# Moving z's parts, batch 1's bounds, a product with u and one half step's preparation in the opening of a squared-ReLU attention with a soft mixture of experts

## The chip, the cores and the metric

One core of one Trainium2 chip runs the whole program. The metric is the device time of one execution in microseconds (us); lower is better. TensorE is called PE, ScalarE ACT, VectorE DVE, GpSimd POOL, and SyncE's queue of transfers SP, as the profile does.

## The reference

Eight batches of 2496 tokens. `u` and `v` have 256 columns, `z` has 64. Attention uses `z` for both queries and keys; its result, times `u`, goes into a soft mixture of experts.

```python
scores = scale * np.matmul(z, z.transpose(0, 2, 1))      # scale = 1/2496
attn = np.maximum(scores, 0.0) ** 2
x = (u * np.matmul(attn, v)).reshape(B * S, D)
logits = x @ phi                                         # 32 slots: 8 experts of 4
# softmax over tokens gives slot inputs, two layers per expert, softmax over slots mixes them back
```

## The kernel before, in words

Attention is cut, batch by batch, into chunks of 512 queries. A chunk is walked in ten **half steps**, each with 256 keys. Half steps are numbered through the run; the loop variable is `h` (line 1094). Half steps 0 to 9 are chunk 0, 10 to 19 chunk 1, 20 to 29 chunk 2. The work of half step k is called sc(k), relu(k) and so on here:

- **sc(k)**: PE multiplies z by z into PSUM. For k below 12 (`RAW_SCORES`) it uses raw z in fp32; from 12 on it uses z's two fp16 parts in three pairs of matmuls, which read high and high, high keys and low queries, low keys and high queries, in this order (lines 407 to 420).
- **relu(k), square(k)** on ACT, out of PSUM into a tile `r`.
- **cast(k)**: the high fp16 part `ph`, on POOL or on ACT; **pl(k)**: the low part, `r - ph`, on DVE. Up to k = 21 both go in two halves.
- **y(k)**: DVE transposes `r` for the mirrored chunk, where scores are needed a second time; those later half steps ("turned") fetch it back from memory and need no sc. Half steps 12, 13, 20, 22 and 23 are turned.
- **sums of k**: PE multiplies `ph` and `pl` by v's two parts into `acc`, as high by high, v's low by high, v's high by low. With a preparation between them the sums of a half step are cut in two phases, p0 and p1 (`sums_halves`); else they are whole (`sums_whole`).

Every engine's instructions stay in the order of the program (`InOrder`, line 72). In half step h (up to 17) the program issues p0 of h, then the preparation of h+2 (scores on PE, then relu, square, cast, pl, y), then whatever lies in the list `behind`, then p1 of h. From 19 on it prepares h+3; 18 prepares both 20 and 21. Between p0 and p1 stands a `nop` on POOL (line 645) that passes PE on.

The names the change touches:

- `z_splits[j]` makes z's parts for block j of batch 0: the high part on ACT, the low part on DVE (lines 161 to 166). `FIRST_Z` (line 49) says at the end of which half step. With `FIRST_MEETS` the half steps of chunk 1 meet the blocks 1, 0, 2, 4, 3, so sc(14) needs blocks 1 and 2, sc(16) block 4, sc(18) block 3.
- `landing[h]` is moved into `behind` in half step h. Batch 1's five bounds (a DVE reduction of z times z into `tops`, line 156) land there, then `add_bounds` (a PE matmul over `tops`) and `factors` (four small DVE instructions on its result).
- `finish_chunk` writes chunk 0's result `xg` from `acc`, then multiplies it by u (line 685).
- `prepare_first` and the lines around 1068 to 1089 order the first preparations by hand; `largest` and `scale_v` make v's factor `v_by`.

Of the kernel before, what the change touches and what calls it, by code (L numbers as in the profile page):

```python
# [8 lines left out]
F32 = mybir.dt.float32  # L9
# [9 lines left out]
P = 128  # L19
# [6 lines left out]
QC = 512  # L26
# [5 lines left out]
NP = KT // 4  # L32
NBLK = 16
NRAW = 12
NW_OWN = 7
# [10 lines left out]
)  # L46
FIRST_MEETS = ((0, 1, 2, 3, 4), (1, 0, 2, 4, 3)) + MEETS[0][2:]

FIRST_Z = {8: 1, 10: 2, 11: 4, 13: 3}

RAW_SCORES = 12

FILL = 6, 3

WHOLE, KEEP = 2, 6

ON_ACT = 3, 5, 7

# [25 lines left out]
def attn_soft_moe_kernel(ctx, tc, uT, v, zz, zh, phi, ww, outT):  # L84
    nc = tc.nc

    pe, act, dve, sp, gp = (InOrder(tc, x) for x in (nc.tensor, nc.scalar, nc.vector, nc.sync, nc.gpsimd))
# [82 lines left out]
    def add_bounds(b, ps, js):  # L170
        ones_k = nc.const_aps.tensor(1.0, [P, P], F32)
        for h, rows in enumerate(HALF if b else [slice(0, P)]):
            pe.matmul(ps[:, h, js], ones_k[rows], tops[b % 2][rows, js], start=True, stop=True)

    def factors(b, ps, js):


        n2, by = (t[b % 2][:, js] for t in (norm2, z_by))
        total = ps[:, 0, js]
        if b:  # L180
            dve.tensor_reduce(n2, ps[:, :, js].rearrange("p h j -> p j h"), axis=AX.X, op=ALU.add)
            total = n2
        dve.tensor_scalar(bits(n2), bits(total), EVEN, None, op0=ALU.bitwise_and)
        dve.tensor_scalar(
            bits(by), bits(n2), EVEN, 1, op0=ALU.bitwise_xor, op1=ALU.logical_shift_right
        )
        dve.tensor_scalar_mul(by, by, 2.0**77)
# [29 lines left out]
    def largest(b):  # L217


        root, w = v_by[b % 2], few[b % 2]  # L220
        n2 = norm2[b % 2].unsqueeze(2).to_broadcast([P, NP, 2])
        dve.tensor_scalar(
            bits(root), bits(energy[b % 2]), 1, ROOT, op0=ALU.logical_shift_right, op1=ALU.bitwise_and
        )
        r2 = root.rearrange("p (j i) -> p j i", i=2)
        dve.tensor_tensor_reduce(
            r2, r2, n2, 1.0, 2.0**-120, op0=ALU.mult, op1=ALU.max, accum_out=w[:, 0:1]
        )
# [78 lines left out]
    ut_ = {}  # L307
# [55 lines left out]
    def run(todo):  # L363
        now, todo[:] = todo[:], []
        for f in now:
            f()
# [99 lines left out]
    def prepare_first(k):  # L466

        r = wa.tile([P, 2, QC], F32, tag="r", name=f"r_{k}", bufs=4)
        pend[k] = hi, lo = high_low(k)
        ps, _ = early.pop(k)  # L470

        def parts(t):
            nc.gpsimd.tensor_copy(hi[:, t], r[:, t])
            return lambda: dve.tensor_sub(lo[:, t], r[:, t], hi[:, t])

        return lambda: relu(k, r, ps), lambda: act.activation(r, r, AF.Square), parts, lambda: stage(k, r)
# [23 lines left out]
    def prepare(k):  # L500

        x = halves[k]
        n = x.ch[2]

        if x.turned:
            whole = arriving.pop(k)
            run(middle)
        else:
            r = wa.tile([P, 2, QC], F32, tag="r", name=f"r_{k}", bufs=4)
            ps, m = early.pop(k) if k in early else scores(k)  # L510
            relu(k, r[:, :, :m], ps[:, :, :m])
            act.activation(r[:, :, :m], r[:, :, :m], AF.Square)
            run(middle)
            whole = r[:, :, :m].rearrange("p h (a r) -> p h a r", r=P // 2 if x.borrows else P)
        run(splitting)
        run(turning)
        cast = gp.tensor_copy
        if x.turned or (k <= CATCH + 3 and x.turns and x.at % 3 and k >= 2 * NP):
            cast = act.copy
        pieces = [(whole, slice(0, P), cast)]  # L520
        if x.borrows:
            lent = arriving.pop(k)
            pieces = [(lent, slice(0, P // 2), act.copy), (whole, slice(P // 2, P), dve.tensor_copy)]

        m = QC if x.padded else n

        def halves_of(t):
            return t[:, :, :m].rearrange("p h (a r) -> p h a r", r=P)

        def high():  # L530
            pend[k] = high_low(k)
            for src, cols, cast in pieces:
                cast(halves_of(pend[k][0])[:, :, :, cols], src)

        def low():
            hc, lc = map(halves_of, pend[k])
            for src, cols, _ in pieces:
                dve.tensor_sub(lc[:, :, :, cols], src, hc[:, :, :, cols])

        if x.borrows:  # L540
            pend[k] = high_low(k)
            hc, lc = map(halves_of, pend[k])
            for src, cols, cast in pieces:
                cast(hc[:, :, :, cols], src)
                dve.tensor_sub(lc[:, :, :, cols], src, hc[:, :, :, cols])
        elif k <= CATCH + 3:
            pend[k] = high_low(k)
            hc, lc = map(halves_of, pend[k])
            for t in range(2):
                cast(hc[:, t], whole[:, t])  # L550
                dve.tensor_sub(lc[:, t], whole[:, t], hc[:, t])
        elif x.turned:
            high()
            low()
        else:
            casting.append(high)
            splitting.append(low)
        if x.turns:
            stage(k, r)
        if x.lends:  # L560
            y = turns_sb.tile([P, 4, 2, 2, NS], F32, tag="yd", name=f"yd_{k}", bufs=1)
            dve.transpose(
                y.rearrange("p a j i q -> p i a j q"),
                r.rearrange("p h (a i q) -> p h a i q", i=4, q=NS)[:, :, :, 2:4],
            )
            stores.append((k - 1, lambda: lend(x, y)))
        run(behind)
# [98 lines left out]
    xg_ = {}  # L666

    def finish_chunk(b, ch, acc):
        j, _, n, t0 = ch
        ut = ut_.pop(t0)  # L670
        s = 0
        while s < n:
            q, o = divmod(t0 + s, 1024)
            w = min(n - s, 1024 - o)
            if q not in xg_:
                xg_[q] = wk.tile([P, 2, 1024], F32, tag="xg", name=f"xg_{q}")
            for c in (slice(0, 1), slice(1, 2)) if t0 + n == N else (slice(0, 2),):
                first = t0 == 0
                dve.scalar_tensor_tensor(
                    xg_[q][:, c, o : o + w], acc[:, c, s : s + w], out_by[b % 2][:, j : j + 1],  # L680
                    kept[0][:, c] if first else ut[:, c, s : s + w],
                    op0=ALU.mult, op1=ALU.add if first else ALU.mult,
                )
                if first:
                    dve.tensor_mul(xg_[q][:, :, 0:w], xg_[q][:, :, 0:w], ut)
            if o + w == 1024:
                work.extend(groups(q))
            s += w
# [258 lines left out]

    def load_u(b, ch):
        _, _, n, t0 = ch
        ut = wa.tile([P, 2, QC], F32, tag="ut", name=f"ut_{t0}", bufs=1)  # L950
        q0 = t0 - b * S
        sp.dma_start(
            ut[:, :, :n], uT[b, :, q0 : q0 + n].rearrange("(c p) q -> p c q", p=P)
        )
        ut_[t0] = ut
# [5 lines left out]
    splits, later = {}, {}  # L961
    for b in range(1, B):
        base, order = (b - 1) * 2 * NP * NQ, BLOCKS[b == B - 1]
        z_at = [28, 29, 30, 31, 39]
        v_from = [6, 7, 8, 9, 24, 25, 26, 31, 32, 33]
        v_sq = [17, 18, 19, 20, 28, 29, 30, 32, 33, 33]
        v_high = [43, 41, 41, 42, 42, 43, 44, 44, 45, 45]
        v_low = [47, 42, 43, 44, 45, 46, 48, 49, 50, 51]
        for i, (j, at) in enumerate(zip(order, z_at)):
            splits.setdefault(base + 9 + 2 * i, []).append((load_z, b, j, [base + 12 + 2 * i, base + at]))  # L970
        for i, (start, *steps) in enumerate(zip(v_from, v_sq, v_high, v_low)):
            splits.setdefault(base + start, []).append((load_v, b, i, [base + at for at in steps]))
        later[base + 23] = lambda b=b: add_bounds(b, next_acc(), slice(0, NP))
        later[base + 24] = lambda b=b: factors(b, accs[-1], slice(0, NP))
        later[base + 36] = lambda b=b: largest(b)
        later[base + 39] = lambda b=b: scale_v(b, ms_ps.tile([P, 2, 512], F32, tag="ms", name=f"mx_{b}"))
    landing, fetched = {}, set()
# [2 lines left out]
    def next_acc():  # L980

        accs.append(acc_ps.tile([P, 2, QC], F32, tag="acc", name=f"acc_{len(accs)}"))
        return accs[-1]
# [87 lines left out]
        first_v[i](act if i in ON_ACT else dve)  # L1071
    square2()
    low2 = [parts2(t) for t in range(2)]
    largest(0)
    sums_raw(1, acc_raw, 0, [1])
    scale_v(0, small)
# [9 lines left out]
    dve.tensor_scalar(  # L1086
        raw_by[:, NP:], z_by[0][:, 1:2], z_by[0][:, 1:2], 2.0**-22, op0=ALU.mult, op1=ALU.mult
    )
    prepare(3)
    kept = [own_w.tile([P, 2, QC], F32, tag="own", name="kept", bufs=NW_OWN)]  # L1090
    landing_kept = lambda: act.activation(kept[0], acc_raw, AF.Identity, scale=2.0**22 / S**2)
    landing[KEEP] = [landing_kept]
# [356 lines left out]
```

## Time and profile before

| | |
|---|---|
| median of 3 runs | 1269.56 us (1269.4 to 1270.18) |
| the profiled execution, its own time | 1269.41 us |
| its span, first to last instruction | 1267.6 us |
| PE busy | 1241.6 us, 98% |
| DVE, ACT, POOL busy | 83%, 66%, 18% |
| granted TensorE clock, mean | 0.987 |

The span leaves 1.8 us of the profiled time outside it. A busy share is an average over stages, and matmul ends in the profile are modelled, so PE's pace is read from the starts of its instructions.

### The profile page before, as it was taken

What the parts mean: (1) busy time and instruction counts of PE and PEld (TensorE: products, weight loads), DVE (VectorE), ACT (ScalarE), POOL (GpSimd) and SP (SyncE); (2) the same over time, 40 slices, a digit from 0 to 9 for tenths busy, and PEclk for the clock granted to TensorE, in tenths of its full rate; (3) what the DMA queues carried; (4) which work ended last, traced back from release to release, by engine and by line L of the source; (5) the groups of instructions that cost most, each with busy time, mean ns of one, the idle gap of its engine ahead of it and who ended that gap; (6) DMA issues with size and microseconds to landing.
All of it is one profiled execution on the core that took longest, in us unless ns stands there. A gap on an engine that the chain in (4) does not pass through costs nothing.

```text
span 1267.6 us, 27769 instructions
## 1 busy us (share of the span) xinstructions
PE 1241.6 (98%) x10936; PEld 604.5 (48%) x10937; DVE 1046.0 (83%) x1468; ACT 841.9 (66%) x1143; POOL 229.3 (18%) x234
## 2 busy tenths in 40 slices
PE   9999999999999999999999999999999999999984
PEld 3444454444544444445544444444444455445752
DVE  7988898779978889788987888788987789776563
ACT  7877765767666766577656776577666777564552
POOL 2211032201311032110311123110321113110100
PEclk9999999999999999999999999999999999999995
DMA  6778469773878748784787758786587848989769
GB/s 197 244 211 277 170 190 303 232 238 119 240 263 270 240 126 274 244 235 163 213 276 218 268 149 244 256 255 210 156 277 230 267 142 239 277 278 328 280 272 376
DMA packets 136690, 299.28 MB, mean 236 GB/s; under 512 B 17904, under 2 KB 38896, under 8 KB 124656
## 3 DMA queue, kind: packets, MB, share of 16 engines
q1 hardware_dynamic: 136560, 297.51, 74.0%
q8 instruction: 86, 1.41, 0.5%
q14 instruction: 44, 0.36, 0.1%
HBM read 162.43 MB, written 113.77 MB: 218 GB/s over the span
## 4 chain that ended last, share of the span: by engine, by line
PE 93%; ACT 2%; DVE 2%; DMA 1%; issue 1%; POOL 0%; ACTq 0%; DVEq 0%; POOLq 0%
PE acc L80 76%; PE sc L80 11%; PE lg L80 3%; DMA outT<-ot 1%; PE pf L80 1%; ACT r L80 1%; ACT ot L80 1%; DVE pl L80 1%; PE h L80 1%; PE po L80 0%; DVE y L80 0%; PE acc_raw L80 0%; DVE v L80 0%; DVE xg L80 0%; PE xt L80 0%
## 5 line engine op out<-in xcount | busy, mean ns | idle before, releaser
L80 PE MATMUL acc<-ph,v 64*128 64x512 f16 (+4 forms) x5004 | 923.7, 368 | 0.4 <-POOLq L80 0.3
L80 PEld LDWEIGHTS <-v 64*128 64x128 f16 (+1 forms) x7506 | 467.7, 95 | 521.3 <-issue 38.6
L80 PE MATMUL acc<-pl,v 64*128 64x512 f16 (+5 forms) x2502 | 597.9, 368 | 2.3 <-DVE pl L80 2.3
L80 DVE TENSOR_TENSOR pl<-r,ph 128x1024 f16<-128x1024 f32 (+1 forms) x428 | 475.7, 1123 | 35.0 <-ACT ph L80 25.6
L80 POOL CAST ph<-r 128x1024 f16<-128x1024 f32 (+1 forms) x210 | 224.4, 1072 | 942.7 <-ACT r L80 693.8
L80 ACT ACTIVATE r<-sc 128x1024 f32<-128x1024 f32 (+1 forms) x233 | 220.3, 946 | 234.5 <-PE sc L80 231.9
L80 DVE STREAM_TRANSPOSE y<-r 128x1024 f32<-128x1024 f32 x160 | 198.3, 1239 | 68.9 <-ACT r L80 65.0
L80 ACT ACTIVATE r<-r 128x1024 f32<-128x1024 f32 (+1 forms) x243 | 239.0, 983 | 7.7
L80 ACT CAST ph<-r 128x1024 f16<-128x1024 f32 (+1 forms) x180 | 172.0, 963 | 98.3 <-PE acc L80 60.0
L80 PE MATMUL sc<-z,z 64*128 64x512 f16 x912 | 123.9, 376 | 0.0
L80 PEld LDWEIGHTS <-z 64*128 64x128 f16 x1380 | 69.7, 94 | 72.1 <-DVE z L80 0.3
L80 DVE SCALAR_TENSOR_TENSOR xg<-acc,out_by,ut 128x1024 f32<-128x1024 f32 (+7 forms) x56 | 50.6, 926 | 17.7 <-PE acc L80 17.4
L80 DVE SCALAR_TENSOR_TENSOR v<-vr,v_by,v 128x512 f16<-128x512 f32 (+1 forms) x81 | 60.6, 750 | 0.0
L80 ACT ACTIVATE v<-vr,v_by 128x512 f16<-128x512 f32 (+1 forms) x81 | 53.8, 707 | 7.6 <-DVE v_by L80 7.6
L80 DVE STREAM_TRANSPOSE yd<-r 128x512 f32<-128x512 f32 x36 | 25.5, 709 | 31.2 <-ACT r L80 29.8
L80 PE MATMUL sc<-z 64*128 64x512 f16 (+1 forms) x468 | 50.6, 321 | 0.0
L80 DVE STREAM_TRANSPOSE y<-xg 128x512 f32<-128x512 f32 x72 | 49.4, 686 | 0.0
L80 ACT ACTIVATE vq<-vr 128x512 bf16<-128x512 f32 x73 | 45.5, 623 | 3.6 <-DMA vr<-in_v 3.3
L80 DVE COPY ot<-pf 128x1024 f32<-128x1024 f32 (+2 forms) x21 | 24.1, 1147 | 18.1 <-PE pf L80 14.6
L80 DVE TENSOR_TENSOR pl<-rd,ph 128x512 f16<-128x512 f32 x36 | 24.7, 686 | 14.9 <-ACT ph L80 14.9
L80 ACT COPY ot<-pf 128x1024 f32<-128x1024 f32 (+2 forms) x21 | 20.0, 951 | 22.8 <-PE pf L80 16.4
L80 DVE SCALAR_TENSOR_TENSOR z<-zr,z_by,z 128x512 f16<-128x512 f32 x35 | 25.8, 737 | 0.0
(193 smaller groups left out, 555.9 us busy)
## 6 DMA issues: line engine op xcount, KB each, us to landing
turned<-y SPq DMA_DIRECT2D x320, 256.0 KB, 5.5
r<-turned SPq DMA_DIRECT2D x76, 1024.0 KB, 7.3
xt<-y SPq DMA_DIRECT2D x288, 72.0 KB, 3.9
vr<-in_v SPq DMA_DIRECT2D x80, 256.0 KB, 4.9
outT<-ot SPq DMA_DIRECT2D x17, 1024.0 KB, 7.0
ut<-in_uT SPq DMA_DIRECT2D x31, 512.0 KB, 6.2
lent<-yd SPq DMA_DIRECT2D x144, 64.0 KB, 3.3
rd<-lent SPq DMA_DIRECT2D x36, 256.0 KB, 4.0
```

The source lines that it names most:

```text
L80: return lambda *a, **k: self.tc.keep_in_program_order(f(*a, **k))
```

## The change

It has four parts. z's parts of blocks 1, 2, 4, 3 are made at the end of half steps 10, 11, 13, 15 instead of 8, 10, 11, 13. Batch 1's bounds land in half steps 21 to 25 instead of 12, 14, 16, 18, 20, with `add_bounds` and `factors` in 26 and 27 instead of 23 and 24. Chunk 0's product with u lands in half step 17 instead of at the end of 9, and its u lies in another pool until then. Half step 3's relu, square and cast are issued before `largest(0)` and `scale_v`.

```diff
-FIRST_Z = {8: 1, 10: 2, 11: 4, 13: 3}
+FIRST_Z = {10: 1, 11: 2, 13: 4, 15: 3}
+FIRST_U = 17
@@ prepare_first
-            nc.gpsimd.tensor_copy(hi[:, t], r[:, t])
+            gp.tensor_copy(hi[:, t], r[:, t])
@@ finish_chunk
                 if first:
-                    dve.tensor_mul(xg_[q][:, :, 0:w], xg_[q][:, :, 0:w], ut)
+                    landing.setdefault(FIRST_U, []).append(
+                        lambda x=xg_[q][:, :, 0:w]: dve.tensor_mul(x, x, ut)
+                    )
@@ load_u
-        ut = wa.tile([P, 2, QC], F32, tag="ut", name=f"ut_{t0}", bufs=1)
+        place, n_bufs = (wa, 1) if t0 else (own_w, NW_OWN)
+        ut = place.tile([P, 2, QC], F32, tag="ut" if t0 else "own", name=f"ut_{t0}", bufs=n_bufs)
@@ the plan of splits
-            splits.setdefault(base + 9 + 2 * i, []).append((load_z, b, j, [base + 12 + 2 * i, base + at]))
+            bound = 21 + i if b == 1 else 12 + 2 * i
+            splits.setdefault(base + 9 + 2 * i, []).append((load_z, b, j, [base + bound, base + at]))
-        later[base + 23] = lambda b=b: add_bounds(b, next_acc(), slice(0, NP))
-        later[base + 24] = lambda b=b: factors(b, accs[-1], slice(0, NP))
+        add_at = 26 if b == 1 else 23
+        later[base + add_at] = lambda b=b: add_bounds(b, next_acc(), slice(0, NP))
+        later[base + add_at + 1] = lambda b=b: factors(b, accs[-1], slice(0, NP))
@@ the opening
     low2 = [parts2(t) for t in range(2)]
+    relu3, square3, parts3, stage3 = prepare_first(3)
+    relu3()
+    square3()
+    low3 = [parts3(t) for t in range(2)]
     largest(0)
@@
-    prepare(3)
+    run(turning)
+    for f in low3:
+        f()
+    stage3()
```

## Rows read from the trace of the kernel before

**Rows 1.** The page: busy time of each engine, and the chain of work that ended last, by engine.

```profile
PE 1241.6 (98%) x10936; PEld 604.5 (48%) x10937; DVE 1046.0 (83%) x1468; ACT 841.9 (66%) x1143; POOL 229.3 (18%) x234
...
PE 93%; ACT 2%; DVE 2%; DMA 1%; issue 1%; POOL 0%; ACTq 0%; DVEq 0%; POOLq 0%
```

**Rows 2.** PE's waits over the whole run, one line: what waited, for what, us in total, times, longest.

```profile
PE acc L80 <- DVE pl L80: 2.3, 6, 0.8
```

**Rows 3.** The timeline around half step 2: start, duration, engine, line, operation, tiles, shapes, count, and in brackets the idle time before and what ended it. In order: v's first parts, relu(3), sc(4), cast(3), and p1 of half step 2.

```profile
16.28 1.52 ACT L80 ACTIVATE v<-vr,v_by 128x256 f16<-128x256 f32 x3 [2.68 <-DVE v_by L80]
...
17.70 1.09 ACT L80 ACTIVATE r<-sc,raw_by 128x1024 f32<-128x1024 f32 x1
...
18.64 1.04 PE L80 MATMUL sc<-cw 64*128 64x512 f32 x4
...
19.95 1.17 POOL L80 CAST ph<-r 128x512 f16<-128x512 f32 x2 [5.11 <-ACT r L80]
...
20.00 0.60 PE L80 MATMUL acc<-ph,v 64*128 64x512 f16 x4 [0.33 <-POOLq L80]
```

**Rows 4.** The timeline of half steps 9 to 12, same columns. In order: sc(11), the high part of z's block 1, relu(11), pl(11), chunk 0's result, its product with u, pl(12), PE's first read of pl(12), the low part of block 2, and the weight load of sc(14) that needs it.

```profile
42.64 1.02 PE L80 MATMUL sc<-cw 64*128 64x512 f32 x4
...
42.86 0.71 ACT L80 ACTIVATE z<-cw,z_by 128x512 f16<-128x512 f32 x1
...
44.08 1.09 ACT L80 ACTIVATE r<-sc,raw_by 128x1024 f32<-128x1024 f32 x1
...
47.16 1.67 DVE L80 TENSOR_TENSOR pl<-r,ph 128x512 f16<-128x512 f32 x2 [0.51 <-POOL ph L80]
...
48.75 1.27 DVE L80 SCALAR_TENSOR_TENSOR xg<-acc,out_by,kept 128x1024 f32<-128x1024 f32 x1
...
50.06 1.22 DVE L80 TENSOR_TENSOR xg<-xg,ut 128x1024 f32<-128x1024 f32 x1
...
51.20 1.28 DVE L80 TENSOR_TENSOR pl<-r,ph 128x512 f16<-128x512 f32 x2
...
51.94 0.39 PE L80 MATMUL acc<-pl,v 64*128 64x512 f16 x2 [0.80 <-DVE pl L80]
...
52.41 0.74 DVE L80 SCALAR_TENSOR_TENSOR z<-cw,z_by,z 128x512 f16<-128x512 f32 x1
...
53.20 0.10 PEld L80 LDWEIGHTS <-z 64*128 64x128 f16 x2 [0.29 <-DVE z L80]
```

**Rows 5.** The timeline of half steps 13 and 14, same columns. In order: sc(15), relu(15), cast(15) on ACT, sc(16), pl(15), the high part of z's block 3, y(15), the low part of block 3.

```profile
56.03 0.83 PE L80 MATMUL sc<-z,z 64*128 64x512 f16 x6
...
56.90 1.02 ACT L80 ACTIVATE r<-sc 128x1024 f32<-128x1024 f32 x1
...
59.04 1.14 ACT L80 CAST ph<-r 128x512 f16<-128x512 f32 x2
...
59.27 0.83 PE L80 MATMUL sc<-z,z 64*128 64x512 f16 x6
...
59.69 1.29 DVE L80 TENSOR_TENSOR pl<-r,ph 128x512 f16<-128x512 f32 x2 [0.20 <-ACT ph L80]
...
60.09 0.72 ACT L80 ACTIVATE z<-cw,z_by 128x512 f16<-128x512 f32 x1
...
60.91 1.24 DVE L80 STREAM_TRANSPOSE y<-r 128x1024 f32<-128x1024 f32 x1
...
62.07 0.71 DVE L80 SCALAR_TENSOR_TENSOR z<-cw,z_by,z 128x512 f16<-128x512 f32 x1
```

**Rows 6.** The timeline of half steps 15 to 19, same columns. In order: sc(17), sc(18), pl(19), PE's first read of pl(19), y(19), pl(20).

```profile
62.51 0.83 PE L80 MATMUL sc<-z,z 64*128 64x512 f16 x6
...
65.78 0.81 PE L80 MATMUL sc<-z,z 64*128 64x512 f16 x6
...
72.96 1.67 DVE L80 TENSOR_TENSOR pl<-r,ph 128x512 f16<-128x512 f32 x2 [0.50 <-POOL ph L80]
...
74.08 0.38 PE L80 MATMUL acc<-pl,v 128*128 128x512 f16 x1 [0.26 <-DVE pl L80]
...
74.55 1.23 DVE L80 STREAM_TRANSPOSE y<-r 128x1024 f32<-128x1024 f32 x1
...
75.72 1.24 DVE L80 TENSOR_TENSOR pl<-r,ph 128x512 f16<-128x512 f32 x2
```

**Rows 7.** The timeline around batch 1's bounds, same columns. In order: the first of the five bounds (half step 12), `add_bounds` (half step 23), sc(29) in half step 26, the last piece of `behind` in half step 25, and DVE's next instruction after it, which belongs to half step 26.

```profile
58.83 0.65 DVE L80 CUSTOM_DVE_ANT_0 sq<-zr 128x512 bf16<-128x512 f32 x1
...
88.48 0.28 PE L80 MATMUL acc<-tops,const-float32-1.0 64*128 64x5 f32 x4
...
97.68 0.49 PE L80 MATMUL sc<-z 64*128 64x256 f16 x6
...
98.93 0.67 DVE L80 STREAM_TRANSPOSE y<-xg 128x512 f32<-128x512 f32 x1
...
99.52 1.18 DVE L80 TENSOR_TENSOR pl<-r,ph 128x1024 f16<-128x1024 f32 x1
```

**Rows 8.** Stretches of 2 us near the end of the run: length, busy time (and count) of each engine, the granted clock (PEclk), DMA share and GB/s.

```profile
1232.00:1234.00 2.00, 1.15 (x21) 0.84 (x24) 1.02 (x2) 0.80 (x1) 0.00 (x0) 1.00 1.00 406
1234.00:1236.00 2.00, 0.43 (x12) 0.05 (x8) 0.86 (x1) 0.80 (x1) 0.00 (x0) 0.96 0.99 406
1236.00:1238.00 2.00, 1.62 (x12) 0.81 (x12) 0.26 (x2) 0.18 (x1) 0.00 (x0) 0.50 1.03 425
```

## The prediction, made before the changed kernel was run

> **What bounds the kernel now.** I read the page first, then the chain that ended last, then PE's waits, and only then the timeline of the opening. PE is busy for 98% of the span and makes up 93% of the chain [rows 1]. So a wait of PE in the middle of the run is paid in full, since no slack behind it gives it back, and a saving elsewhere counts only where PE waits today. PE's waits on pl, the commonest kind before the last stage, are 2.3 us in all, in six places [rows 2]. That caps what the change can win: the waits of the opening are p1 of half step 2 (0.33 us, for a nop on POOL queued behind cast(3) [rows 3]), pl(12) (0.80 us [rows 4]), z's block 2 (0.29 us [rows 4]) and pl(19) (0.26 us [rows 6]). Together they are 1.7 us. Against that stands whatever the moved work delays.
>
> To see that, I looked at how far ACT and DVE are ahead of PE, and they are not. relu(15) starts 0.04 us after sc(15) ends (56.03 + 0.83, then 56.90), and the rest of step 15's preparation follows it in a chain: ACT's cast at 59.04, pl(15) at 59.69, y(15) at 60.91 [rows 5]. PE meanwhile does the sums and issues sc(16) 3.24 us after sc(15) [rows 5]. Work placed at the end of half step 13 comes behind that whole chain on ACT and DVE, and reaches them after PE has come to sc(16). PE does 15 pairs of matmuls in these 3.24 us, 0.216 us a pair; a 128-row matmul of the same width counts as one pair.
>
> **Half step 3 ahead.** ACT was idle for 2.68 us until v_by came at 16.28 [rows 3]; relu(3) and square(3) need 1.09 and about as much again, so they fit, and v's first parts are not delayed. cast(3) then runs some 4 us earlier, the nop is no longer behind it, and p1 of half step 2 no longer waits: 0.33 us won. Unseen is what the cast costs DVE when it overlaps pl(2): pl takes 1.67 us under a POOL cast and 1.28 under an ACT cast [rows 4], so 0 to 0.2 us for one half of it. I take PE 0.33 us earlier up to sc(11), with 0.1 and 0.5 as the ends.
>
> **z's blocks 1 and 2, and the product with u, out of half steps 8 to 12.** Block 1's high part, 0.71 us, leaves ACT ahead of relu(11). relu(11) came 0.42 us after sc(11) ended (43.66, then 44.08 [rows 4]); it now comes 0.1 after, and with the 0.33 at 43.4. pl(11) followed it 3.08 us later, so now at about 46.5. From there DVE goes on without a break: pl(11) 1.59, chunk 0's result 1.31, pl(12) 1.21 (all start to start [rows 4]). The product, 1.14 us, is gone, so pl(12) comes at 49.4 and PE does not wait for it. But then come block 1's low part (0.7), pl(13) (1.2, as pl(12)), and only then block 2's low part: 46.5 + 1.59 + 1.31 + 1.21 + 0.7 + 1.2 = 52.5. It started at 52.41 before, and sc(14)'s last pair followed 0.79 us later [rows 4]. So at sc(14) PE stands where it stood: what was saved is waited for there. I take 0, with -0.4 and +0.3 as the ends.
>
> **Block 4 for sc(16).** Its parts take exactly the slot that block 3's have today: high on ACT at 60.09, behind cast(15), low on DVE at 62.07, behind y(15) [rows 5]. The bound that goes from 58.83 [rows 7] does not bring this forward, since pl(15) waited 0.20 us for the cast anyway [rows 5]. From sc(15) to the low part is 62.07 - 56.03 = 6.04 us; with 0.79 to the weight load, sc(16)'s last pair comes 6.83 us after sc(15). Unhindered it came 3.24 + 0.43 = 3.67 after. **+3.16 us.** Less than 1.4 it cannot be: even the high part ends at 60.8, 1.5 after sc(16)'s start. Behind the waiting matmuls stand p1 of 14 and everything after it on PE, and relu(16).
>
> **Block 3 for sc(18).** It is the same chain, from sc(17): relu, square, cast on ACT, pl, y, low part, 6.83 us. Today sc(18)'s last pair is 65.78 - 62.51 + 0.43 = 3.70 after sc(17) [rows 6]. **+3.13 us.**
>
> **pl(19).** Without the bound of half step 16, POOL's cast and pl(19) come some 0.25 us earlier against sc(18), and PE's 0.26 us of wait [rows 6] goes. **-0.26 us.**
>
> **The product with u in half step 17.** It lands on DVE behind y(19) and ahead of pl(20). PE asks for pl(20) one half step, twelve matmuls or 2.59 us, after its read of pl(19): 74.08 + 2.59 = 76.67. pl(20) starts at 75.72 [rows 6] and is readable 0.74 later (as pl(12), 51.20 to 51.94 [rows 4]), at 76.46: a margin of 0.21 us. The product takes 1.14 of DVE there. **+0.9 us**, ends 0 and 1.14.
>
> **Bounds and add_bounds.** Five bounds of some 0.66 us go to a stretch where DVE has idle time, and they cost nothing themselves. But add_bounds in half step 26 waits on the bound of half step 25, where before it stood three half steps behind the last one. PE issues sc(29) at 97.68 and comes to add_bounds 0.33 us later, at 98.0. DVE does the last piece of `behind` of half step 25 at 98.93 and would start the bound where its next instruction stands now, at 99.52 [rows 7]; it is read at 100.2. **+2.2 us**, ends 1.5 and 2.4. p1 of 26 stands behind it. factors, a half step later still, holds nobody.
>
> The load of chunk 0's u keeps its place on SP, and chunk 1's no longer waits for the product; no one waited for either. The cast through the ordered queue changes nothing else.
>
> **The sum**: 0 + 3.16 + 3.13 - 0.26 + 0.9 + 2.2 = +9.1 us against the profiled execution's 1269.41, that is 1278.5. The median of the runs shown is 0.15 higher, which I leave aside.
>
> **The clock.** It stood at 1.00, the 2.4 GHz level, until PE's work thinned out near the end: it fell to 0.50, the 1.2 GHz level, at the end of a stretch in which PE was busy 0.43 of 2 us [rows 8]. The waits at sc(16) and sc(18) are alike: two pairs of matmuls, 0.43 us, in some 3.3 us. At 1.2 GHz a half step's 2.59 us of sums take twice that, so a fall that holds for one half step costs up to 2.6 us, and at both places 5.2. The Trainium skill, TensorE: Matmul & The Clock Gate (Part 1), has the clock fall after a stretch in which PE idled; as the z waits are broken by matmuls, they would by its word leave the clock alone and the sum at +9.1, while the fall near the end came with PE still at work. So the row speaks for a fall and the page against one.
>
> **Rivals.** *The clock falls too* at one or both z waits: 1279.8 to 1283.7. For it speaks [rows 8]; against it, that PE is at full work right before and after. *Only z is late*: the product hides in a margin that I have too small, and the bound of half step 25 is done in time, because DVE is less loaded in half steps 20 to 25 than today: 1269.41 + 3.16 + 3.13 - 0.26 = 1275.4. Against it: y(28), which the bound follows, hangs on sc(28), not on DVE's load. *ACT and DVE get ahead of PE.* Freed of the product and five bounds, some 4.4 us of DVE work, they would lead PE by a half step through chunk 1; from a lead of 3.2 us on, all the new waits go, as do the old ones of 1.7 us: 1267.7. Against it: relu(k) cannot precede sc(k), and ACT already starts it 0.04 us after; the lead can't be built from DVE's relief.
>
> **Chances.** As summed: 0.50, with a range of its own from 1276.5 to 1279.7 by the ends above. With a falling clock: 0.27. Only z late: 0.15. Ahead of PE: 0.08. What a measurement tells from no change is about 0.2%, or 2.5 us; the first three cases lie above that, the last on either side of it: slower 0.92, within 0.03, faster 0.05. The range goes from below the third case to the middle of the clock's: 1274.5 to 1282.5.
>
> **What would show it.** Right: p1 of half step 2 directly behind sc(4), without POOL's nop; relu(11) 0.1 us after sc(11); PE waits on DVE z of about 1.6 us at sc(14) and, in two pieces (ACT's high part, DVE's low part), some 3 us at sc(16) and at sc(18); a wait of about 1 us on pl(20); one of about 2 us at add_bounds on DVE's tops. Wrong, if sc(16) and sc(18) keep 3.24 us of distance to the score before; if the product lies where DVE is idle; or if add_bounds starts right behind sc(29). PEclk below 1.00 within the first 80 us would be the clock's case.

## The result and the profile after

The changed kernel took 1279.95 us (median of 5 runs, 1279.87 to 1282.34), against 1269.56 us for the kernel before (5 runs, 1268.49 to 1270.18). The ratio is 1.0086, with an interval from 1.0075 to 1.0097: 0.9% slower, 1.45 us above the time forecast and inside its range. The profiled execution is one of the slower ones, 1281.26 us with a span of 1279.5.

The page of the kernel after: span, busy times, and the chain that ended last by engine.

```profile
span 1279.5 us, 27766 instructions
...
PE 1245.0 (97%) x10936; PEld 605.6 (47%) x10937; DVE 1045.2 (82%) x1468; ACT 842.2 (66%) x1143; POOL 229.7 (18%) x234
...
PE 91%; DVE 4%; ACT 2%; DMA 2%; issue 1%; POOL 0%; SPq 0%; ACTq 0%; DVEq 0%; POOLq 0%
```

Against [rows 1], PE does the same 10936 matmuls, yet is busy 3.4 us longer, and the chain runs through DVE for 4% instead of 2%. The first says that some of the matmuls ran slower. The second says that PE now stands behind DVE. What it stands behind is in the next view.

PE's waits from 0 to 140 us of the kernel after: what waited, for what, us in total, times, longest. The last line is that for pl over the whole run.

```profile
PE sc L82 <- DVE z L82: 4.0, 3, 1.4
PE sc L82 <- ACT z L82: 3.0, 2, 1.6
PE acc L82 <- DVE tops L82: 2.0, 1, 2.0
PE acc L82 <- DVE few L82: 0.9, 1, 0.9
...
PE acc L82 <- DVE pl L82: 0.5, 1, 0.5
PE acc L82 <- DVE v L82: 0.3, 1, 0.3
...
PE acc L82 <- DVE pl L82: 1.5, 4, 0.5
```

The first three kinds, 9.0 us, were not there before. On the other side, the waits for pl fell over the whole run from 2.3 us [rows 2] to 1.5. The wait for `few`, in the first microseconds, is 0.2 us longer, and the one for v takes the place of the 0.33 for POOL [rows 3]. That makes 9.0 - 0.8 + 0.2 = 8.4 us of waits; with 3.4 us of slower matmuls it is 11.8, and the span grew by 11.9.

To place this, I numbered PE's instructions in both traces and took the difference of their starts: how late PE is, place by place. A minus means early. A cost is the step from one row to the next, since an execution can already start late or early (the first row). The first two columns are two profiled executions of the change, the second from the chip of a later experiment (`after_b`). The other columns belong to experiments below.

| PE late by (us), at | after | again | filled | no_z | no_bounds | no_u | z_only | bounds_only | best2 |
|---|---|---|---|---|---|---|---|---|---|
| p1 of 2 | 0.12 | -0.09 | 0.16 | 0.11 | -0.20 | -0.06 | -0.12 | 0.14 | -0.79 |
| read of pl(12) | -1.19 | -1.39 | -1.15 | -0.87 | -1.51 | -0.55 | -0.60 | 0.14 | -2.10 |
| sc(14), last pair | 0.21 | 0.00 | 0.24 | -0.86 | -0.12 | 1.29 | 1.24 | 0.14 | -2.10 |
| sc(16), last pair | 3.34 | 3.13 | 3.37 | -0.86 | 3.01 | 4.42 | 4.37 | 0.14 | -2.10 |
| sc(17) | 3.35 | 4.83 | 3.38 | -0.86 | 4.71 | 6.12 | 5.85 | 0.14 | -2.10 |
| sc(18), last pair | 6.44 | 7.91 | 6.47 | -0.88 | 7.79 | 9.20 | 8.94 | 0.14 | -2.35 |
| sc(19) | 7.77 | 9.31 | 6.48 | -0.88 | 9.15 | 10.77 | 8.95 | 0.14 | -2.18 |
| read of pl(19) | 7.35 | 8.89 | 6.21 | -1.14 | 8.73 | 10.35 | 8.95 | -0.11 | -2.45 |
| read of pl(20) | 8.01 | 9.55 | 7.09 | -0.26 | 9.39 | 10.36 | 8.95 | -0.11 | -2.45 |
| sc(29) | 7.87 | 9.41 | 6.95 | -0.40 | 9.39 | 10.22 | 8.95 | -0.25 | -2.45 |
| p1 of 26 | 10.26 | 11.80 | 9.36 | 1.99 | 9.39 | 12.61 | 8.95 | 2.14 | -2.45 |
| half step 28 | 11.95 | 13.49 | 9.36 | 3.68 | 9.39 | 12.61 | 8.95 | 2.14 | -2.45 |
| end of the span | 11.85 | 14.25 | 11.79 | 4.93 | 9.28 | 13.43 | 11.46 | 2.34 | -1.24 |

In the first column most of the loss comes at five places: 3.13 us at sc(16), 3.09 at sc(18), 1.33 behind sc(18) on the way to sc(19), 2.39 between sc(29) and p1 of 26, and 1.69 behind that. Three of them are waits of PE; in the two that stand behind sc(18) and behind p1 of 26, PE waits for nobody.

The timeline of half steps 10 to 14 of the kernel after: start, duration, engine, line, operation, tiles, shapes, count, and in brackets the idle time before and what ended it. In order: the low part of block 1, sc(14), the low part of block 2, sc(14)'s last pair, sc(15), relu(15), cast(15), the high part of block 4, sc(16) up to its last pair, y(15), the low part of block 4, that last pair.

```profile
50.78 0.74 DVE L82 SCALAR_TENSOR_TENSOR z<-cw,z_by,z 128x512 f16<-128x512 f32 x1
...
51.61 0.59 PE L82 MATMUL sc<-z,z 64*128 64x512 f16 x4
...
52.64 0.74 DVE L82 SCALAR_TENSOR_TENSOR z<-cw,z_by,z 128x512 f16<-128x512 f32 x1
...
53.44 0.39 PE L82 MATMUL sc<-z,z 64*128 64x512 f16 x2 [1.24 <-DVE z L82]
...
56.26 0.81 PE L82 MATMUL sc<-z,z 64*128 64x512 f16 x6
...
57.11 1.02 ACT L82 ACTIVATE r<-sc 128x1024 f32<-128x1024 f32 x1
...
59.26 1.14 ACT L82 CAST ph<-r 128x512 f16<-128x512 f32 x2
...
60.30 0.72 ACT L82 ACTIVATE z<-cw,z_by 128x512 f16<-128x512 f32 x1
...
61.07 0.61 PE L82 MATMUL sc<-z,z 64*128 64x512 f16 x4 [1.41 <-ACT z L82]
61.12 1.24 DVE L82 STREAM_TRANSPOSE y<-r 128x1024 f32<-128x1024 f32 x1
...
62.28 0.71 DVE L82 SCALAR_TENSOR_TENSOR z<-cw,z_by,z 128x512 f16<-128x512 f32 x1
...
63.05 0.39 PE L82 MATMUL sc<-z,z 64*128 64x512 f16 x2 [1.37 <-DVE z L82]
```

Against [rows 5]: cast(15), y(15) and the two parts behind them stand 0.2 us from where they stood, each on its old slot. The parts are now block 4's, and sc(16) needs them at once. From sc(15) to sc(16)'s last pair are 6.79 us, where 6.83 were forecast. sc(14)'s last pair comes within 0.3 us of its old time [rows 4], though pl(12) was read 1.2 us sooner.

The two losses in which PE waits for nobody show in the granted clock. Stretches of 2 us of the kernel after: length, busy time and count of PE, PEld, DVE, ACT, POOL, PEclk, DMA share, GB/s.

```profile
60.00:62.00 2.00, 0.61 (x4) 0.11 (x4) 2.00 (x3) 1.02 (x2) 0.00 (x0) 1.00 0.00 0
62.00:64.00 2.00, 0.95 (x10) 0.48 (x12) 0.99 (x2) 0.52 (x1) 0.00 (x0) 1.00 0.37 83
64.00:66.00 2.00, 2.00 (x22) 0.89 (x20) 0.00 (x0) 1.56 (x2) 0.29 (x1) 1.00 0.96 201
...
70.00:72.00 2.00, 0.61 (x4) 0.11 (x4) 2.00 (x4) 0.62 (x1) 0.00 (x0) 0.99 0.92 369
72.00:74.00 2.00, 1.35 (x8) 0.53 (x10) 0.59 (x1) 0.70 (x1) 0.00 (x0) 0.50 0.99 366
74.00:76.00 2.00, 2.00 (x16) 0.78 (x14) 0.00 (x0) 1.94 (x4) 0.00 (x0) 0.66 0.92 240
...
106.00:108.00 2.00, 0.04 (x2) 0.00 (x0) 2.00 (x5) 1.74 (x3) 0.54 (x1) 1.00 0.91 293
108.00:110.00 2.00, 1.98 (x18) 1.01 (x20) 2.00 (x3) 0.00 (x0) 0.00 (x0) 0.88 0.96 362
110.00:112.00 2.00, 2.00 (x12) 0.81 (x10) 1.36 (x3) 0.00 (x0) 0.00 (x0) 0.50 1.01 366
```

0.50 is the 1.2 GHz level. It follows the wait at sc(18) (0.61 of 2 us busy) and the wait at `add_bounds` (0.04 of 2), and PE, busy for the whole of 110 to 112, issues 12 matmuls there; in `bounds_only` below it does 22 in 2 us behind the same wait, at 1.00. Behind the wait at sc(16), 60 to 66 us, the clock stayed at 1.00 in this execution. In the second column, the same program, it fell there too: 1.70 us from sc(16) to sc(17).

### The profile page after: what moved, and what is told of

Same layout as the page of the kernel before. It is cut to its first block, busy times and chain, and to the rows that moved or that the text cites. A ratio compares the mean times of both kernels' runs of the same rounds, so it can differ in the third digit from the quotient of the medians.

```text
span 1279.5 us, 27766 instructions
## 1 busy us (share of the span) xinstructions
PE 1245.0 (97%) x10936; PEld 605.6 (47%) x10937; DVE 1045.2 (82%) x1468; ACT 842.2 (66%) x1143; POOL 229.7 (18%) x234
## 4 chain that ended last, share of the span: by engine, by line
PE 91%; DVE 4%; ACT 2%; DMA 2%; issue 1%; POOL 0%; SPq 0%; ACTq 0%; DVEq 0%; POOLq 0%
PE acc L82 74%; PE sc L82 11%; PE lg L82 3%; PE pf L82 1%; DVE pl L82 1%; DMA outT<-ot 1%; ACT r L82 1%; DVE y L82 1%; ACT ot L82 1%; PE h L82 1%; PE po L82 1%; DMA vr<-in_v 0%; DMA cw<-in_zz 0%; DVE v L82 0%; DVE xg L82 0%
```

## The experiments

My theory after the result: the sum of the prediction holds term by term except at the opening, and about one fall of the clock lies on top of it in the median run. The rivals: the loss at the z waits is the clock's alone; the parts of the change depend on one another, so that none of them can be priced by itself; the clock's fall costs nothing that the waits don't cost already. `no_z`, `no_bounds`, `no_u` and `filled` share a chip; `after_b`, `filled_b`, `relu3_u_only` and `best` a second; `lead`, `z_only`, `bounds_only` and `best2` a third. Each is compared with runs of the kernel before on its own chip (medians 1269.68, 1269.96 and 1269.72 us).

**z's parts put back** (`no_z`).

```diff
-FIRST_Z = {10: 1, 11: 2, 13: 4, 15: 3}
+FIRST_Z = {8: 1, 10: 2, 11: 4, 13: 3}
```

> The changed kernel with z's parts back at the end of half steps 8, 10, 11, 13; the other three parts stay. Theory (each late wait is paid by PE in full, and only z is late at sc(14), sc(16), sc(18)): the waits at sc(16) and sc(18), 3.12 and 3.09 us in the changed kernel's trace, go, with the fall of the clock behind sc(18); sc(14) comes about 0.9 us earlier than in the kernel before, as the product with u is out of DVE's way. Left are the wait on pl(20) (0.5), the one at add_bounds (2.0) and the clock's fall behind it (up to 1.8): 1271 to 1273 us. Rival (the two waits only take the place of waits that would come anyway some half steps later): 1276 us or more.

Measured: 1272.05 us (10 runs, 1270.93 to 1274.93), ratio 1.002 [1.0011, 1.0029]. PE's waits from 0 to 140 us of this kernel:

```profile
PE acc L82 <- DVE tops L82: 2.0, 1, 2.0
PE acc L82 <- DVE pl L82: 1.1, 3, 0.7
```

No wait for z is left, and sc(16) and sc(18) add nothing in the table. Moving z's parts is thus the largest cost of the change, about 8 of its 10 us, the falls of the clock behind these waits included. The rest, pl(20) and `add_bounds`, stands (0.88 and 2.39 us), and the clock fell behind `add_bounds` (1.7 us from p1 of 26 to half step 28).

**z's parts alone, on the kernel before** (`z_only`): the same line, the other way round.

```diff
-FIRST_Z = {8: 1, 10: 2, 11: 4, 13: 3}
+FIRST_Z = {10: 1, 11: 2, 13: 4, 15: 3}
```

> The kernel before with z's parts alone moved to the end of half steps 10, 11, 13, 15. Theory: block 2's low part comes behind the product with u as well, so sc(14) is about 1.2 us late; sc(16) and sc(18) 3.1 each; nothing at pl(20), nothing at add_bounds: +7.4 us and one or two falls of the clock at 1.3 to 1.8 each: 1278 to 1281. Rival (without the other parts the waits are hidden): under 1274.

Measured: 1280.5 us (4 runs, 1278.36 to 1281.69), ratio 1.0084 [1.007, 1.0097]. The waits of this kernel:

```profile
PE sc L80 <- DVE z L80: 4.2, 3, 1.5
PE sc L80 <- ACT z L80: 3.0, 2, 1.6
...
PE acc L80 <- ACT ph L80: 0.8, 1, 0.8
```

By its time the z move alone is as slow as the whole change, within the noise. The trace says that its own price is smaller. At half step 28 it is 8.95 us late, 1.48 of them for a fall of the clock behind sc(16), so its waits cost about 7.5 us, as expected; the kernel after is 11.95 late there. In this execution PE then lost 2.51 us more later in the run, which the kernel after did not. The last line above belongs to that: a wait at 1183 us for a cast of ACT, which had itself waited for a transfer of a turned `r`. At sc(14) the z move alone is dearer than the full change (1.24 us late instead of 0.21), since the product with u is still in the way there.

**Bounds put back** (`no_bounds`).

```diff
-            bound = 21 + i if b == 1 else 12 + 2 * i
+            bound = 12 + 2 * i
...
-        add_at = 26 if b == 1 else 23
+        add_at = 23
```

> The changed kernel with batch 1's bounds, add_bounds and factors back in half steps 12 to 24; the other three parts stay. Theory: PE's wait at add_bounds (2.0 us) and the fall of the clock behind it (up to 1.8) go, pl(19) is read about 0.3 us later again: 1276 to 1278 us. Rival (only z costs, the wait at add_bounds is taken back later): 1279.5 to 1280.5, as the changed kernel.

Measured: 1279.78 us (4 runs, 1278.68 to 1281.47), ratio 1.0083 [1.0067, 1.0098]: above what I expected, and by the time alone this run says nothing. Its trace does. The wait at `add_bounds` is gone (p1 of 26 as late as sc(29), 9.39 us), but the clock fell behind both z waits here. The first of them:

```profile
60.00:62.00 2.00, 0.60 (x4) 0.11 (x4) 2.00 (x4) 0.69 (x2) 0.00 (x0) 1.00 0.00 0
62.00:64.00 2.00, 1.28 (x8) 0.52 (x10) 0.66 (x2) 0.85 (x1) 0.00 (x0) 0.78 0.53 117
64.00:66.00 2.00, 2.00 (x12) 0.77 (x10) 0.00 (x0) 1.23 (x2) 0.61 (x2) 0.50 0.97 225
```

The wait is the one of the kernel after (0.60 us of matmuls in that stretch, there 0.61), and there no fall followed. So whether the clock falls at a given wait changes from execution to execution, as the first two columns show for one and the same program.

**Bounds alone, on the kernel before** (`bounds_only`).

```diff
+            bound = 21 + i if b == 1 else 12 + 2 * i
...
+        add_at = 26 if b == 1 else 23
```

> The kernel before with batch 1's bounds alone moved to half steps 21 to 25, add_bounds and factors to 26 and 27. Theory: pl(19) 0.26 us earlier, add_bounds 2.3 late, and behind it a fall of the clock in some executions, up to 1.7: +2.0 to +3.7, 1271.5 to 1273.5. Rival (the wait at add_bounds needs the delays of the other parts): 1269.5.

Measured: 1273.13 us (7 runs, 1271.74 to 1273.6), ratio 1.0026 [1.0015, 1.0037]. `add_bounds` and the stretches around it:

```profile
99.90 0.39 PE L80 MATMUL acc<-tops,const-float32-1.0 64*128 64x5 f32 x4 [1.98 <-DVE tops L80]
```

```profile
98.00:100.00 2.00, 0.10 (x2) 0.10 (x2) 2.00 (x5) 1.70 (x3) 0.41 (x1) 1.00 1.07 390
100.00:102.00 2.00, 2.00 (x22) 1.05 (x24) 1.97 (x4) 0.00 (x0) 0.00 (x0) 1.00 0.96 373
```

PE loses 2.39 us at p1 of 26 and saves 0.14 where `add_bounds` stood before and 0.25 at pl(19). In this execution the clock did not fall, and it is the fastest of the seven, with a mean clock of 0.988. The other six have 0.984 to 0.986 and lie 1.2 to 1.9 us above it, which fits a fall in each; without a profile of them that isn't shown.

**The product with u put back** (`no_u`).

```diff
-                    landing.setdefault(FIRST_U, []).append(
-                        lambda x=xg_[q][:, :, 0:w]: dve.tensor_mul(x, x, ut)
-                    )
+                    dve.tensor_mul(xg_[q][:, :, 0:w], xg_[q][:, :, 0:w], ut)
```

> The changed kernel with chunk 0's product with u back at the end of half step 9; the other three parts stay. Theory: DVE's product (1.14 us) stands again ahead of pl(12) and block 2's low part, so sc(14) is 1.1 us later, and the wait on pl(20) (0.5 to 0.7) goes: 0.5 us slower than the changed kernel, about 1280.4. Rival (the product in half step 17 is the cost, and in 9 it hides): 0.6 us faster, about 1279.3.

Measured: 1283.04 us (4 runs, 1279.05 to 1286.79), ratio 1.0104 [1.0083, 1.0124], 2.6 us above what I expected. sc(14) came 1.08 us later than in the kernel after, and the loss at pl(20) was gone (0.01 instead of 0.66). So moving the product pays 1.1 us at sc(14) and costs 0.7 to 0.9 at pl(20). In the profiled execution the clock fell behind both z waits (1.70 and 1.57 us) and not behind `add_bounds`; at half step 28 it is 0.66 us later than the kernel after. The rest of the excess, in four runs that lie 7.7 us apart, is not explained.

**The waits filled with matmuls** (`filled`, `filled_b`). The kernel after, with matmuls of ones whose result nobody reads, put into the three long waits (nine more at the head of `add_bounds`). It does this work on top of all the rest.

```diff
+        if b == 1:
+            idle_work(9)
...
+                if k in WAITS and i in (0, 2):
+                    idle_work(WAITS[k][i // 2])
...
+    WAITS = {16: (6, 6), 18: (7, 6)}
+
+    def idle_work(n):
+        ps = ms_ps.tile([P, 2, 512], F32, tag="ms", name="idle")
+        for _ in range(n):
+            pe.matmul(ps[:, 0], ones[:, 0:P], ones, start=True, stop=True)
```

> The changed kernel, all four parts, with matmuls of ones into an unused PSUM tile where PE waits: 6 and 6 at sc(16), 7 and 6 at sc(18), 9 ahead of add_bounds, 0.216 us each, so a little less than the waits they stand in. The result does not use them. Theory (the waits cost 8.8 us and the fall of the clock behind them the rest): the granted clock stays at 1.00 up to the end's stretch, mean 0.987, and the time is 1278.3 us in all executions. Rival (the clock has no part in it, or falls for another reason): 1279.9 us or more, with a spread of 2 us as in the changed kernel.

Measured: 1281.2 us (5 runs, 1278.67 to 1284.96), ratio 1.0094 [1.0078, 1.011]; 1278.3 was expected. In the opening the expectation held. Three of the stretches shown above, in this kernel:

```profile
70.00:72.00 2.00, 2.00 (x12) 0.61 (x10) 2.00 (x4) 0.65 (x2) 0.00 (x0) 1.00 0.92 381
72.00:74.00 2.00, 2.00 (x18) 0.72 (x18) 0.62 (x1) 0.89 (x1) 0.00 (x0) 1.00 0.97 353
...
110.00:112.00 2.00, 2.00 (x17) 0.77 (x14) 0.47 (x1) 1.38 (x2) 0.00 (x0) 1.00 0.98 311
```

The clock stays at 1.00, and the table shows what that is worth: sc(16) and sc(18) are as late as in the kernel after, but nothing is lost behind sc(18), and half step 28 comes 9.36 us late instead of 11.95. But later in the run 2.4 us went elsewhere. PE's waits of the whole run hold a line that neither the profiled execution of before nor that of after has:

```profile
PE sc L82 <- ACT r L82: 1.7, 1, 1.7
```

It stands at 722 us, and ACT had waited there for transfers of v and of a turned `r`. A rival is that the filling itself brings such late waits; `z_only`, which fills nothing, lost 2.51 us late in the run as well, so they come without it. Since the total missed, I repeated the pair, unaltered and filled, on another chip.

> The changed kernel again, unaltered, as the measure for the kernel with filled waits on the same chip. Theory: the waits cost 8.8 us, and each fall of the clock behind one of them (in the earlier profile behind sc(18) and behind add_bounds) 1.3 to 1.8 us more: 1278.3 plus that for each fall, 1279.5 to 1282.5, and the more the lower the mean granted clock. Rival (the clock has no part): times without relation to the clock.

> The kernel with filled waits again. In its first profile the clock did not fall in the opening, but PE waited 2.5 us later in the run, in half step 228's neighbourhood at 722 us, for ACT, which had waited for transfers; so its time said little. Theory: without such a wait 1278.3 to 1279, clock 0.987 or more, 1.5 us or more below the changed kernel beside it. Rival (filling does not help, the late wait belongs to it): no faster than the changed kernel beside it.

Measured: 1282.01 us unaltered (4 runs, 1279.97 to 1283.66, mean clock 0.983 to 0.986), 1280.55 us filled (5 runs, 1279.46 to 1281.45, 0.987 to 0.988). Filled is 1.46 us shorter, but the intervals of the ratios (1.0078 to 1.0106 and 1.0067 to 1.0094) overlap, so the times alone don't show that filling helps. The traces are clearer than the times: three falls in the unaltered kernel, at the sc(17), sc(19) and half step 28 rows of the table's second column, and none in the opening of the filled one, which again lost 2.2 us later on (1.2 of them in a wait at 1016 us).

**Only half step 3 and the product** (`relu3_u_only`): the kernel after with z and the bounds both put back.

```diff
+FIRST_Z = {8: 1, 10: 2, 11: 4, 13: 3}
...
+            bound = 12 + 2 * i
...
+        add_at = 23
```

> The kernel before with two of the four parts alone: half step 3's relu, square and cast ahead of v's factor, and the product with u in half step 17. z's parts and batch 1's bounds stay as before. Theory (the late z parts and the late bounds are all of the loss): sc(14) comes 0.9 us earlier as in the run with z's parts back, pl(20) waits 0.9 behind the product: 1269 to 1270.5, the same as before, and the clock does not fall in the opening. Rival (one of these two parts costs as well): 1271 or more.

Measured: 1269.69 us (11 runs, 1268.63 to 1271.44), ratio 0.9998 [0.9989, 1.0007]: no difference. What the product wins by pl(12), 0.95 us, is given back at pl(20), 0.87. Together with `z_only` and `bounds_only` this splits the change in three, and the parts add up: at half step 28 `z_only` is 8.95 us late, less 1.48 for its fall of the clock behind sc(16), `bounds_only` 2.14, this kernel -0.07. That makes 9.54 us, and the whole change with no fall, `filled`, is 9.36 late there. The parts can thus be priced each by itself, to within some 0.3 us.

**A shorter delay** (`lead`): blocks 4 and 3 one half step sooner than in the change, bounds one sooner.

```diff
-FIRST_Z = {10: 1, 11: 2, 13: 4, 15: 3}
+FIRST_Z = {10: 1, 11: 2, 12: 4, 14: 3}
...
-            bound = 21 + i if b == 1 else 12 + 2 * i
+            bound = 20 + i if b == 1 else 12 + 2 * i
```

> The changed kernel with one half step more of lead: block 4's parts at the end of half step 12 instead of 13, block 3's at the end of 14 instead of 15, the bounds in 20 to 24 instead of 21 to 25 (add_bounds stays in 26). Nothing else differs. Theory (PE waits because these pieces stand behind a preparation that itself hangs on the score just before): the waits at sc(16), sc(18) and add_bounds go, all but some tenths, and so do the falls of the clock; the wait for block 2 at sc(14) and the one on pl(20) stay: +0.9, that is 1269.7 to 1271. Rival (it is the amount of work that ACT and DVE have in these half steps, not the order): most of the loss stays, 1274 or more.

Measured: 1271.88 us (11 runs, 1270.27 to 1273.94), ratio 1.0017 [1.0009, 1.0026]. sc(16) and sc(18) in this kernel:

```profile
59.99 0.81 PE L82 MATMUL sc<-z,z 64*128 64x512 f16 x6
...
66.44 0.59 PE L82 MATMUL sc<-z,z 64*128 64x512 f16 x4
...
67.75 0.39 PE L82 MATMUL sc<-z,z 64*128 64x512 f16 x2 [0.71 <-DVE z L82]
...
100.03 0.28 PE L82 MATMUL acc<-tops,const-float32-1.0 64*128 64x5 f32 x4
```

One half step is enough for block 4 and for the bounds, since neither sc(16) nor `add_bounds` waits. For block 3 it isn't. PE comes to sc(18)'s last pair 6.9 us after sc(16) (66.44 + 0.43 - 59.99) and does it 7.76 us after; the 0.71 in brackets is most of that wait. The chain from sc(16) is longer than the 6.83 us forecast for the others: relu(16) starts 0.55 us after sc(16) ends, behind cast(15) on ACT, and pl(16) takes 1.67 us beside POOL's cast where pl(15) took 1.30. The median is about 0.9 us above the range that I expected; in the profiled execution 0.6 of that stood already at p1 of half step 2, ahead of all that differs in it.

**What can be kept** (`best`, `best2`). Both put only block 1 later (half step 9), make chunk 0's result and its product in half step 11, spread the bounds over 12 to 21 with `add_bounds` in 24, and make cast(3) on ACT instead of POOL. In `best` half of cast(3) stands ahead of v's first parts, in `best2` all of it behind them.

```diff
+FIRST_Z = {9: 1, 10: 2, 11: 4, 13: 3}
+FIRST_U = 11
...
+            (act.copy if k == 3 else gp.tensor_copy)(hi[:, t], r[:, t])
...
+            bound = (12, 14, 18, 20, 21)[i] if b == 1 else 12 + 2 * i
...
+        add_at = 24 if b == 1 else 23
...
```

> A version with each part where DVE or ACT has room: block 1's z parts at the end of half step 9, the others as before; chunk 0's result and its product with u both in half step 11, behind pl(13); the bounds in 12, 14, 18, 20, 21 with add_bounds in 24; half step 3 ahead of v's factor with its cast on ACT, in two halves, so that POOL does not run beside pl(2). Theory: PE's waits for pl in the opening and for block 2 go: 0.3 at half step 2, 1.35 up to sc(14), 0.3 at pl(19): 1267.5 to 1268. Rival (PE is held by something the profile does not name, and the waits return as others): 1269.5.

Measured: 1269.41 us (11 runs, 1267.81 to 1270.09), ratio 0.9992 [0.9983, 1.0001]: no difference, where 1267.5 to 1268 was expected. The half of cast(3) on ACT held up v's parts; a wait of PE in this kernel:

```profile
PE acc L82 <- ACT v L82: 0.6, 1, 0.6
```

> The version with each part where there is room, once more, with both halves of cast(3) on ACT behind v's first parts instead of one ahead of them: in the version before, v's first parts came 0.6 us late behind that cast. Theory: p1 of half step 2 comes 0.3 us earlier than in the kernel before, sc(14) 1.6 earlier, pl(19) 0.3: 1.5 to 2 us faster than before up to batch 2, 1267.5 to 1268.5 in the median if no wait for transfers comes later in the run. Rival (the opening hangs on when v's transfers land): no better than the version before, about 0.5 us faster than the kernel before.

Measured: 1268.19 us (11 runs, 1267.54 to 1269.84), ratio 0.9991 [0.9982, 1.0]. PE is 2.45 us ahead at half step 28. Of this 0.79 stood at p1 of half step 2 already, where runs differ by themselves, and 1.21 is lost again later. The median is 1.5 us lower, but the interval touches 1, so I don't call it faster.

## Why the prediction was right, and where not

The kind of loss, its places and its size without the clock were right. The `filled` kernel has the sum with no fall in it: 9.36 us at half step 28, of which 0.16 stood at p1 of half step 2, against the 9.1 forecast. By steps:

- **Block 4 for sc(16)**: 3.13 us for 3.16. **Block 3 for sc(18)**: 3.09 for 3.13. The chain relu, cast, pl, y, low part kept its length.
- **sc(14)**: lost 1.4 us there, won 1.3 before; the term of 0 was right. The product alone shows in `no_u`, where 1.08 us comes back.
- **pl(19)**: -0.27 in `filled` for -0.26; `bounds_only` has -0.25, so it is the bounds' doing, as the step said. But a second cause does the same: `no_bounds` wins 0.42 us there. So do the other three executions of the table in which the clock fell behind sc(18), while `z_only`, with the same wait at sc(18), the old bounds and no such fall, wins nothing. While PE is slow there, ACT and DVE catch up: in `no_bounds` pl(19) starts 3.74 us after sc(19), in the kernel before 4.37.
- **The product in half step 17**: 0.88 us in `filled`, 0.66 in the kernel after, for 0.9.
- **Bounds and `add_bounds`**: 2.39 us at p1 of 26, and 0.14 won where `add_bounds` had stood: 2.25 for 2.2.
- **Half step 3 ahead failed**: 0.33 us forecast, none seen. This had no weight in the sum, as its gain was to be waited for at sc(14) anyway. The step said that v's first parts are not delayed, since ACT had room. ACT had; the delay came from POOL and DVE.

The timeline around half step 2 of the kernel after, in order: cast(3), the first half of pl(2), PE's read of v's low part, p1 of half step 2.

```profile
15.88 1.18 POOL L82 CAST ph<-r 128x512 f16<-128x512 f32 x2 [0.84 <-ACT r L82]
...
16.50 1.11 DVE L82 TENSOR_TENSOR pl<-r,ph 128x512 f16<-128x512 f32 x1
...
18.06 0.39 PE L82 MATMUL acc<-ph,v 64*128 64x512 f16 x2 [0.34 <-DVE v L82]
...
20.12 0.61 PE L82 MATMUL acc<-ph,v 64*128 64x512 f16 x4
```

The nop no longer holds p1, as forecast. But cast(3) now runs beside pl(2), which takes 1.11 us. v's low part follows it on DVE, and PE waits 0.34 us for that instead. I had allowed 0 to 0.2 for the overlap, and forgot that v's low part is queued behind it. In `best2`, cast(3) is on ACT and runs beside the other half of pl(2):

```profile
17.40 0.68 DVE L82 TENSOR_TENSOR pl<-r,ph 128x512 f16<-128x512 f32 x1
17.42 1.12 ACT L82 CAST ph<-r 128x512 f16<-128x512 f32 x2
```

Beside ACT it takes 0.68 us. So the price is POOL's: 0.43 us for one half, and not the 0.2 that I took as half of 1.67 - 1.28. The trace of the kernel before already had it: of the two halves of pl(11) [rows 4] the first took 1.07 us beside POOL's cast and the second 0.68 beside ACT's alone, and pl(12), with its 1.28, had no cast beside it. So 1.67 - 1.28 was the price of one half. The Trainium skill, SBUF — State Buffer ("Who interferes with whom"), says that a DVE instruction with two inputs in SBUF contends with a GpSimd instruction that reads SBUF. The row beside POOL's cast, 1.11 us, agrees.

**The rivals.** That the clock falls too came true on top of the likeliest case, so its chance of 0.27 was too small: in each of the two profiled executions of the change it fell, twice and three times, and the median lies 0.25 us above the range that the likeliest case had for itself. That range was also drawn too wide by 0.4 at its upper end: its own ends, 9.13 + 0.3 + 0.24 + 0.2, give 1279.3 and not 1279.7. The whole range held because it took in half of the clock's case. That case looked for a fall at the z waits alone; the one behind `add_bounds` it had at nothing, and it cost 1.69 us.

The price of a fall was too high as well: not 2.6 us but 1.3 to 1.7, as the table's steps behind sc(16), sc(18) and p1 of 26 show. I had reckoned a whole half step at half speed. The profiled execution holds 1.33 + 1.69 = 3.0 us of it, of which some 0.4 came back by sc(29), as pl(19) and pl(20) then waited less; at half step 28 it is 2.6 us behind `filled`.

The median, 1279.95, is 1.2 above 1269.56 + 9.36 less the start's 0.16 (1278.8), about one fall; as the executions without a profile show only a mean clock, that share is argued, not shown, and a late wait for transfers could stand in its place.

The prediction took from the Trainium skill, TensorE: Matmul & The Clock Gate (Part 1), that the clock falls after a stretch in which PE idled, and read this so that waits broken by matmuls would leave the clock alone. The rows of 70 to 76 us above and of 60 to 66 us in `no_bounds` decide against that reading: four matmuls stood in the 2 us of each wait that are shown, and the clock fell. [rows 8] had been the better guide.

That only z is late, or that ACT and DVE get ahead, is refuted: `add_bounds` waited 2.0 us, and relu(15) still starts 0.04 us after sc(15) ends (56.26 + 0.81, then 57.11).

## What to carry to other kernels

When work that PE needs is moved to a later place on an engine that runs in step with PE, its price is the length of the chain that it now stands behind, less the time that PE needs to get there. Both are in the timeline of the kernel before: here 6.83 and 3.67 us gave 3.16, and 3.13 were measured. Up to that distance a delay costs nothing (block 4 one half step later was free, two half steps cost 3 us). The chain has to be measured for the very step: block 3 one half step later, in `lead`, cost 0.9 us, since its chain was longer there. A new wait of PE can also bring a fall of the clock behind it, which is priced by itself.

## What the runs showed of the hardware that I had not expected

- The granted clock fell to 0.50 behind waits in which PE still did 0.6 us of matmuls in 2 us, and behind a single wait of 2.0 us; each fall cost 1.3 to 1.7 us. The same wait brought it in one execution and not in the next: the one at sc(16) in `after_b` and `no_bounds` but not in the kernel after, the wait for tops in the kernel after but not in `bounds_only`. With matmuls in the waits (2.00 of 2 us busy from 70 us on) it stayed at 1.00 there in both profiled executions.
- A subtraction of 128x512 on DVE took 1.11 us beside casts on POOL, 0.68 beside casts on ACT.
- Some executions lose 0.7 to 2.5 us behind half step 28. In the two whose waits I followed back, `filled` at 722 us and `z_only` at 1183 us, ACT had waited for transfers. The profiled execution of after lost nothing there. These losses are one reason why a gain of 2.45 us in the opening of `best2` could not be told from no change in its time.
